# A weight load put behind a transposing transfer, and one group of transposes moved one block earlier, in a fused attention and MLP kernel

## The chip, the cores and the metric

The kernel runs on one core of one Trainium2 chip. Its time is the device time of one launch in microseconds, the median of several runs. The core has five engines that run side by side, each through its own instructions in order: PE (TensorE: matmuls, with weight loads shown apart as PEld), DVE (VectorE), ACT (ScalarE), POOL (GpSimd) and SP (SyncE, here only an issuer of transfers). Transfers are issued from SP's and POOL's queues (a few from ACT's) and carried by 16 DMA engines that all queues share. An engine waits for another engine, or for a transfer, on a semaphore.

## The reference

```python
def _attn_ref(q, k, v, f):
    scores = scale * np.matmul(q, k.transpose(0, 1, 3, 2))
    log_f = np.log(np.clip(f, 0.0001, 1.0))
    cum = np.cumsum(log_f, axis=-1)
    decay = cum[:, :, :, None] - cum[:, :, None, :]
    scores = np.where(causal, -1000000000.0, scores + decay)
    scores = scores - np.max(scores, axis=-1, keepdims=True)
    attn = np.exp(scores)
    attn = attn / (np.sum(attn, axis=-1, keepdims=True) + 1e-09)
    return np.matmul(attn, v)
...
def _moe_ref(x, w_in, w_out):
    h = x @ w_in
    g = 0.5 * h * (1.0 + erf(h * inv_sqrt2))
    return g @ w_out
...
x = attn_out.transpose(0, 2, 1, 3).reshape(B * S, H * D)
return _moe_ref(x=x, **moe_kwargs)
```

q, k and v are (8 batches, 8 heads, 576 tokens, 64 columns) in float32, f is (8, 8, 576). w_in is 512 x 2048 and w_out 2048 x 512. The output has 4608 x 512 numbers in float32. So it is a causal attention with a decay for each token, followed by two matrix products with a gelu between them.

## The kernel before

The kernel goes through the eight batches in order, and works on the heads in four pairs (i = 0 to 3). Within a batch it forms scores for a pair in four tiles in PSUM (`scores`, L299; the matmuls are L319), exponentiates each tile on ACT (L329), masks diagonal blocks on POOL (L331), multiplies by the weighted v (`attend`, L350) and normalizes on DVE (L365, L366). The result, transposed, is xT, the input of the first matrix product. That product (`gemm1`, L437) makes 16 blocks of 128 hidden columns, four matmuls each, and ACT's gelu (L457) turns each into a tile g. The second product (g times w_out, L481, L530, L566 and L590) is spread as filling between the scores of the following batch.

The order is written out by hand: the instructions of an engine stand in the order in which the Python code calls them.

w_out lies in one tile, w_out_sb, loaded in four quarters of 512 KB from POOL's queue (`load_w_out(c)`, L186 to L188). Quarter c holds row blocks 4c to 4c + 3 of the 16. The second product of batch 0 reads blocks 0 to 7 during batch 1's attention (L566), and blocks 8 to 15 at the start of batch 2's attention (L590, in `gemm2_second`).

q and k of batch 0 and batch 1 are transposed by PE (`transposes_first`, L226), 36 small transposes for each pair, and DVE copies the results out of PSUM (L241) into qT and kT. From batch 2 on, transposing transfers issued by SP do it (`transpose_dma`, L255): four for a batch, q and k for heads 0 to 3, then q and k for heads 4 to 7. They write the tiles tq and tk, from which DVE copies (`untangle`, L269) into qT and kT. Behind batch 2's four transfers stand, on SP's queue, the small transposing transfer of batch 1's tail (L422) and the five loads of batch 2's v (L134).

`behind(t, h)` (L613 to L616) puts a small POOL copy that reads one column of t on POOL's queue. POOL waits in it until t has been written, and what POOL issues after it can't start before. The kernel uses it to hold the loads of w_out's quarters 2 and 3 until the k of batch 2 has been loaded.

The places that the change touches are in `second_attention` (batch 1's attention, L912 to L974) and in the loop over batches (L976 to L1013), where batch 0's gemm1 blocks 4 to 9 run with other work put between them. Blocks 10 to 15 of batch 0 are done in batch 1's attention (`gemm1_hold`, L462). Batch 1's first scores need pair 0 transposed. ACT loads another function table when it goes from gelu to exp: a tiny activation at L925, put ahead of the first exp, takes that load. Scores go through two PSUM buffers (pool s_psum), so the third tile waits for the first tile's exp.

Of the kernel before, what the change touches and what calls it, by code (L numbers as in the profile page):

```python
# [18 lines left out]
H = 8  # L19
# [35 lines left out]
def kernel(  # L55
# [130 lines left out]
    def load_w_out(c):  # L186
        kt = slice(c * n_ff // 4, (c + 1) * n_ff // 4)
        nc.gpsimd.dma_start(w_out_sb[:, kt, :], w_out_r[:, kt, :])  # L188
# [28 lines left out]
    def transposes_first(b, i, pool, tag, both=(0, 1), parts=1):  # L217

        half, g = divmod(2 * i, H // 2)
        src = qk_of[b][half]  # L220
        pss = {w: pool.tile([P, J0, D], BF16, tag=tag, name="ps_f") for w in both}
        for j in range(J0):
            for which in both:
                rows = slice(which * D, (which + 1) * D)
                for h in range(2):
                    nc.tensor.transpose(  # L226
                        pss[which][h * D : (h + 1) * D, j, :],
                        src[rows, g + h, j * D : (j + 1) * D],
                        ident_bf[rows, rows],
                    )  # L230

        for which in both:
            dst = (qT, kT)[which][i].rearrange("d (p j) -> d p j", j=J0)
            ps = pss[which].rearrange("d j p -> d p j")
            copies = [nc.vector.tensor_copy] * parts
            if b == i == 0:
                copies = [nc.vector.tensor_copy, nc.scalar.copy]
            n = D // len(copies)
            for at, copy in enumerate(copies):
                part = slice(at * n, (at + 1) * n)  # L240
                copy(dst[:, part], ps[:, part])  # L241

    tq_of = {}
# [39 lines left out]
    def weigh_v(b, i, eng=nc.gpsimd, n0=0, n1=NBLK):  # L283

        hs = slice(2 * i, 2 * i + 2)
        bh = b * H + 2 * i
        w = wT[:, n0:n1, bh : bh + 2].rearrange("p n h -> p h n")
        eng.tensor_tensor(  # L288
            vw(b)[:, hs, n0:n1, 0:D],
            v_sb[:, hs, n0:n1, :],  # L290
            w.unsqueeze(3).to_broadcast([P, 2, n1 - n0, D]),
            Alu.mult,
        )
        if b:
            eng.tensor_copy(vw(b)[:, hs, :, D], w)
# [47 lines left out]
    def attend(b, i, h, ms, pool=o_psum, tag="o"):  # L343
        if (b, i, h) not in o_of:
            o_of[b, i, h] = pool.tile([P, NBLK, D + 1], FP32, tag=tag, name="o")
        o = o_of[b, i, h]
        for m in ms:
            for n in range(m + 1):
                t, c = where(n, m)
                nc.tensor.matmul(  # L350
                    o[:, m, :],
                    e_of[b, i, t][:, h, c : c + P],
                    vw_of[b][:, 2 * i + h, n, :],
                    start=(n == 0),
                    stop=(n == m),
                )

    def normalize(b, i, h):
        if (b, i) not in x_of:
            x_of[b, i] = x_pool.tile([P, NBLK, 2, D], BF16, tag="x", name="x")  # L360
        divide(x_of[b, i][:, 0:NQ, h, :], o_of[b, i, h], NQ)
# [57 lines left out]
    def tail_end(b, o):  # L419
        x = x_pool.tile([P, HP, D], BF16, tag="xt", name="xt")  # L420
        divide(x, o, HP)
        nc.sync.dma_start_transpose(  # L422
            tails[:, :, b].rearrange("d i a t -> d i (a t)"),
            x.rearrange("p k d -> p (k d)"),
        )
# [36 lines left out]
    def gemm1_hold(ffb, copy=nc.vector.tensor_copy):  # L462
        ps = gemm1(0, ffb, act=False)
        h_of[ffb] = h_pool.tile([P, TC], FP32, tag=f"h{ffb}", name=f"h{ffb}")
        copy(h_of[ffb], ps)
# [92 lines left out]
    def gemm2_first(c):  # L558

        pss = [  # L560
            m_psum.tile([P, d_model], FP32, tag="m", name="ps2") for _ in range(2)
        ]
        for kq in (0, 4):
            for ts in range(2):
                for kt in range(kq, kq + 4):
                    nc.tensor.matmul(  # L566
                        pss[ts],
                        g_of[c][kt][:, ts * P : (ts + 1) * P],
                        w_out_sb[:, kt, :],
                        start=(kt == 0),  # L570
                        stop=(kt == 7),
                    )
                    if kt == 7:
                        ot_of.append(
                            o_pool.tile([P, d_model], FP32, tag="ot", name="ot")
                        )
                        copy = nc.scalar.copy if ts else nc.vector.tensor_copy
                        copy(ot_of[ts], pss[ts])
                    yield
# [27 lines left out]
    def take(gen, n):  # L607
        for _ in range(n):
            if next(gen, "end") == "end":
                return  # L610


    def behind(t, h):  # L613

        g = x_pool.tile([P, 1], FP32, tag="gate", name="gate")
        nc.gpsimd.tensor_copy(g[:PT], t[:PT, h, 0:1])  # L616
# [295 lines left out]
    def second_attention():  # L912


        b, fill = 1, gemm2_first(0)

        def av(i, h):
            attend(b, i, h, range(NQ))
            normalize(b, i, h)

        def transposes(i, pool, tag):
            transposes_first(b, i, pool, tag)


        nc.scalar.activation(warm[0:1, 0:1], warm[0:1, 0:1], Act.Exp)  # L925
        def tiles(i, t):
            scores(b, i, t)
            scores(b, i, t + 1)

        def run(i):  # L930
            av(i, 0)
            av(i, 1)

        tiles(0, 0)
        transposes(1, o_psum, "o")
        gemm1_hold(10)
        gemm1_hold(11)
        tiles(0, 2)
        gemm1_hold(12, nc.scalar.copy)
        transposes(2, o_psum, "o")  # L940
        tiles(1, 0)
        gemm1_hold(13)
        run(0)
        tiles(1, 2)
        gemm1_hold(14, nc.scalar.copy)
        transposes(3, o_psum, "o")
        weigh_v(1, 2)
        tiles(2, 0)
        gemm1_hold(15)
        run(1)  # L950
        weigh_v(1, 3)
        tiles(2, 2)
        take(fill, 4)
        tiles(3, 0)
        transpose_dma(2, 0, 4)
        transpose_dma(2, 4, 8)
        to_xT(b, 0, nc.vector.tensor_copy, o_psum, "o")
        to_xT(b, 1, nc.vector.tensor_copy, o_psum, "o")
        take(fill, 4)
        tiles(3, 2)  # L960
        behind(qk_of[2][1], H - 1)
        load_w_out(2)
        load_w_out(3)
        run(2)
        take(fill, 4)
        av(3, 0)
        take(fill, 4)
        both = s_psum.tile([P, 2, 1024], BF16, tag="s", name="ps_x2")
        to_xT(b, 2, nc.scalar.copy, ps=both[:, 0, 0:TC])
        av(3, 1)  # L970
        o = tail(1)
        gemm1_begin(1, both)
        tail_end(1, o)
        load_v(2)  # L974

    for b in range(B):  # L976
        if b == 0:
            first_attention()
        elif b == 1:
            second_attention()  # L980
        else:
            attention(b)
        for ffb in range(4 if b < 2 else 5, n_ff):
            if b == 0 and ffb in HELD:
                continue
            aside = ffb in (8, 9, 12, 13) if b > 1 else b == 1 and ffb % 4 < 2
            if b < 2 or ffb > 6:
                gemm1(b, ffb, ps=spare() if aside else None)
            if b == 1 and ffb % 2 == 0:
                at = HELD[(ffb - 4) // 2]  # L990
                gelu(0, at, h_of[at])
            if b == 0:
                if ffb == 4:
                    attend_tail()
                if ffb == 5:
                    tail_0()
                if ffb == 7:
                    weigh_v(1, 0)
                    load_w_out(0)
                    weigh_v(1, 1)  # L1000
                    load_w_out(1)
                    load_qk_tokens(2)
                if ffb == 8:
                    transposes_first(1, 0, o_psum, "o")
            elif b + 1 < B:
                if b == 1 and ffb == 10:
                    load_qk_tokens(3)
                first, gap = (5, 3) if b == 1 else (1, 4)
                at, late = divmod(ffb - first, gap)
                if late == 0:  # L1010
                    untangle(b + 1, at)
                if late == gap - 2 and (b > 1 or at < 2):
                    weigh_v(b + 1, at)  # L1013
# [34 lines left out]
```

## Time and profile before

| | us |
|---|---|
| median of 3 runs (lowest, highest) | 329.01 (328.47, 330.38) |
| the profiled execution's own time | 330.34 |
| its span, from first to last instruction | 328.4 |
| PE busy | 316.2 |
| ACT busy | 202.5 |
| DVE busy | 176.3 |
| POOL busy | 153.6 |
| PE waiting for other engines or transfers in total, as its table of waits lists them | 7.1 |

All times in the profile count from the start of the span. A timeline row gives the start, the duration, the engine, the line of the code, the operation, the tiles that it writes and reads, the number of instructions merged into the row, and in brackets the time that the engine sat idle before it with what ended that idle time. SPq rows are transfers being issued by SP; their length is the time that SP's queue was held by the issue, not the transfer. The time "to landing" runs from the start of the issue until the data are there. Two tables used for the stage are these: the landing times of w_out's four loads (from the view of that tile), and of tq and tk. They are, as least, median and greatest: 6.5, 7.8 and 10.8 us for w_out_sb, 3.5, 4.0 and 11.2 for tq, 3.5, 3.8 and 7.7 for tk.

The granted TensorE clock is full throughout the span.

### The profile page before, as it was taken

The page shows a single profiled execution, that of the slowest core. Times are in us where ns is not written, and L with a number is a line of the kernel's source. Part 1 is how long each engine was busy: PE and PEld are TensorE (multiplying, and loading weights), DVE is VectorE, ACT ScalarE, POOL GpSimd, SP SyncE. Part 2 cuts the span into 40 slices and gives each one's busy share as a digit, 9 for nine tenths or more (in the row PEclk, how much of TensorE's full clock was granted, in tenths as well). Part 3 has the DMA queues.
Part 4 walks back from the last instruction along what each step waited for, and adds up shares of the span by engine and source line. Part 5 has one row for each costly group of instructions (what it writes and reads, how often), then busy time and mean ns, then how long its engine had stood idle before and what let it go on. Part 6 is the DMA issues. An engine that isn't in the chain of part 4 may idle for free.

```text
span 328.4 us, 8109 instructions
## 1 busy us (share of the span) xinstructions
PE 316.2 (96%) x3308; PEld 168.5 (51%) x3338; DVE 176.3 (54%) x423; ACT 202.5 (62%) x296; POOL 153.6 (47%) x283
## 2 busy tenths in 40 slices
PE   7889999999999999999999999999999989999995
PEld 3664555444464466445644564456545554444443
DVE  5851656763389437982599159914995360010011
ACT  4886885984635895289718980899088916405600
POOL 8987873039306582577336841595059500000000
PEclk9999999999999999999999999999999999999999
DMA  7999999979866959595949683979460141021013
GB/s 122 193 195 219 210 194 146 170 153 173 186 152 166 188 129 135 151 195 104 188 104 212 120 183 76 219 129 188 99 179 2 66 98 40 2 89 38 0 45 85
DMA packets 72294, 43.87 MB, mean 134 GB/s; under 512 B 50081, under 2 KB 65697, under 8 KB 72257
## 3 DMA queue, kind: packets, MB, share of 16 engines
q0 software_dynamic: 18592, 21.89, 38.1%
q1 hardware_dynamic: 53264, 20.93, 29.8%
q8 instruction: 26, 0.43, 0.5%
q10 hardware_dynamic: 400, 0.52, 0.4%
q14 instruction: 12, 0.09, 0.1%
HBM read 36.85 MB, written 9.44 MB: 141 GB/s over the span
## 4 chain that ended last, share of the span: by engine, by line
PE 89%; DMA 4%; ACT 2%; DVE 2%; issue 2%; POOL 0%; SPq 0%; POOLq 0%; DVEq 0%
PE ps L437 38%; PE ps L530 26%; PE ps L481 8%; PE s L319 6%; PE o L350 4%; DMA xT<-x 3%; PE s L640 1%; ACT e L645 1%; PE o L410 1%; PE ps_f L226 1%; DMA q<-in_k_dram 1%; PE ps L590 1%; ACT e L329 1%; DVE x L366 1%; PE ps L566 1%
## 5 line engine op out<-in xcount | busy, mean ns | idle before, releaser
L457 ACT ACTIVATE g<-ps 128x512 bf16<-128x512 f32 x138 | 75.3, 619 | 86.2 <-PE ps L437 85.1
L437 PE MATMUL ps<-xT,w_in_sb 128*128 128x512 bf16 x498 | 112.7, 379 | 2.9 <-DMA xT<-x 1.5
L530 PE MATMUL ps<-w_out_sb,g 64*128 64x512 bf16 (+1 forms) x754 | 104.5, 376 | 0.3
L329 ACT ACTIVATE e<-s 128x896 bf16<-128x896 f32 x112 | 87.8, 836 | 13.2 <-PE s L319 10.9
L437 PEld LDWEIGHTS <-w_in_sb 128*128 128x128 bf16 x576 | 55.1, 98 | 67.9 <-DVE ot L902 2.0
L331 POOL TENSOR_SCALAR_AFFINE_SELECT e<-e 128x256 bf16<-128x256 bf16 (+1 forms) x135 | 48.5, 382 | 29.3 <-ACT e L329 29.2
L530 PEld LDWEIGHTS <-g 64*128 64x128 bf16 (+1 forms) x766 | 42.3, 94 | 30.9
L288 POOL TENSOR_TENSOR vw<-v_sb,wT 128x640 bf16<-128x640 f32 (+1 forms) x30 | 38.0, 1270 | 34.7 <-DMA v_sb<-in_v_dram 31.2
L544 DVE COPY ot<-ps 128x512 f32<-128x512 f32 x20 | 13.8, 692 | 61.5 <-PE ps L530 61.5
L269 DVE COPY kT<-tk 64x288 bf16<-64x288 bf16 x96 | 40.3, 420 | 2.1 <-DMA tk<-k 0.5
L319 PE MATMUL s<-qT,kT 64*128 64x256 bf16 (+1 forms) x336 | 37.8, 275 | 0.8 <-DVE kT L241 0.6
L269 DVE COPY qT<-tq 64x288 bf16<-64x288 bf16 x96 | 34.6, 360 | 3.5 <-DMA tq<-q 2.1
L490 DVE COPY ot<-ps 128x512 f32<-128x512 f32 (+2 forms) x9 | 5.7, 632 | 50.3 <-PE ps L481 50.3
L134 POOL DMA_DIRECT2D v_sb<-in_v_dram x36 | 31.0, 871 | 2.2 <-POOL gate L616 0.8
L319 PEld LDWEIGHTS <-kT 64*128 64x128 bf16 x336 | 18.1, 94 | 20.0 <-issue 4.4
L481 PE MATMUL ps<-w_out_sb,g 128*128 128x512 bf16 (+2 forms) x142 | 27.9, 355 | 0.1
L550 DVE TENSOR_TENSOR ot<-ot,ps 128x512 f32<-128x512 f32 x28 | 19.3, 688 | 4.1 <-remote 2.1
L481 PEld LDWEIGHTS <-g 128*128 128x128 bf16 x144 | 13.5, 98 | 14.5
L350 PEld LDWEIGHTS <-e 128*128 128x128 bf16 x560 | 18.6, 98 | 3.9 <-issue 2.1
L616 POOL CAST gate<-xT 96x1 f32<-96x1 bf16 x5 | 1.3, 267 | 39.8 <-DMA xT<-x 39.8
L350 PE MATMUL o<-vw,e 128*128 128x65 bf16 x560 | 19.8, 194 | 0.2 <-POOL e L331 0.2
L366 DVE TENSOR_TENSOR x<-o,r 128x256 bf16<-128x256 f32 x41 | 17.4, 425 | 1.4
(92 smaller groups left out, 215.1 us busy)
## 6 DMA issues: line engine op xcount, KB each, us to landing
out_dram<-ot SPq DMA_DIRECT2D x32, 256.0 KB, 2.3
v_sb<-in_v_dram POOLq DMA_DIRECT2D x20, 256.0 KB, 4.6
q<-in_q_dram POOLq DMA_DIRECT2D x6, 576.0 KB, 7.6
k<-in_k_dram POOLq DMA_DIRECT2D x6, 576.0 KB, 9.6
v_sb<-in_v_dram POOLq DMA_DIRECT2D x22, 128.0 KB, 5.9
w_in_sb<-in_moe_w_in_dram POOLq DMA_DIRECT2D x4, 512.0 KB, 7.5
w_out_sb<-in_moe_w_out_dram POOLq DMA_DIRECT2D x4, 512.0 KB, 7.8
v_sb<-in_v_dram SPq DMA_DIRECT2D x4, 256.0 KB, 4.1
```

The costliest lines, as they stand in the source:

```text
L134: eng.dma_start(v_sb[p0:P, h0:h1, n, :], v[b, h0:h1, K0[n] + p0 : K0[n] + P].rearrange("h p d -> p h d"),)
L269: nc.vector.tensor_copy(rows[:, odd], src[odd * D : (odd + 1) * D, 2 * i + h].rearrange("d j p -> d p j"),)
L288: eng.tensor_tensor(vw(b)[:, hs, n0:n1, 0:D], v_sb[:, hs, n0:n1, :], w.unsqueeze(3).to_broadcast([P, 2, n1 - n0, D]), Alu.mult,)
L319: nc.tensor.matmul(to, *ab, start=half < 0, stop=half == 1 or not masked)
L329: nc.scalar.activation(et[:, :, z:c], st[:, :, z:c], Act.Exp, scale=scale)
L331: nc.gpsimd.affine_select(out=et[:, :, c0 + z : c0 + P], in_=et[:, :, c0 + z : c0 + P], compare_op=Alu.is_ge, fill=0.0, base=z, pattern=[[ ...
L350: nc.tensor.matmul(o[:, m, :], e_of[b, i, t][:, h, c : c + P], vw_of[b][:, 2 * i + h, n, :], start=(n == 0), stop=(n == m),)
L366: nc.vector.tensor_tensor(x, o[:, 0:n, 0:D], r[:, 0:n].unsqueeze(2).to_broadcast([P, n, D]), Alu.mult,)
L437: nc.tensor.matmul(ps, w_in_sb[:, kt, ffb * P : (ffb + 1) * P], xT(c)[:, kt, 0:TC] if c < B else tails[:, kt % 2, :, kt // 2, :], start=(k ...
L457: nc.scalar.activation(g_of[c][ffb], ps, Act.Gelu)
L481: nc.tensor.matmul(pss[ts][:, c0:c1], g_of[c][kt][:, ts * P : (ts + 1) * P], w_out_sb[:, kt, c0:c1], start=(kt == 0), stop=(kt == n_ff - 1),)
L530: nc.tensor.matmul(banks[r], g_of[c][kt][rows, ts * P : (ts + 1) * P], w_out_sb[rows, kt, :], start=kt == 0, stop=last if r else kt == n_f ...
```

## The change

One line is added in `second_attention`: after quarter 2 of w_out has been issued, a `behind` on the last heads of batch 2's tk, ahead of quarter 3. In the batch loop a condition is taken out, so that the transposes of batch 1's pair 0 stand after block 7 of batch 0's gemm1 (and after the POOL work listed there), and no longer after block 8.

```diff
         tiles(3, 2)
         behind(qk_of[2][1], H - 1)
         load_w_out(2)
+        behind(tq_of[2][1].rearrange("d h j p -> d h (j p)"), H - 1)
         load_w_out(3)
         run(2)
...
                     weigh_v(1, 1)
                     load_w_out(1)
                     load_qk_tokens(2)
-                if ffb == 8:
                     transposes_first(1, 0, o_psum, "o")
             elif b + 1 < B:
```

`tq_of[2]` is the pair of tiles (tq, tk) of batch 2, so `tq_of[2][1]` is tk, and its heads 4 to 7 are written by the last of the four transposing transfers.

In the built programs the instructions are otherwise the same: POOL has one more copy (the gate); SP's later transfer into tk (batch 3's) gets a wait for that copy; on PE the 36 transposes stand ahead of the four matmuls of block 8 where they stood behind them. The second `behind` waits for the one semaphore of that transposing transfer, and PE's first matmul with row block 12 waits for the semaphore of quarter 3 alone.

## The prediction

> **What bounds the kernel now.** I read first the page's busy times and its chain of waits, then the table of what TensorE (PE) waited for, then each engine's timeline at the two edited places.
>
> ```profile
> PE 316.2 (96%) x3308; PEld 168.5 (51%) x3338; DVE 176.3 (54%) x423; ACT 202.5 (62%) x296; POOL 153.6 (47%) x283
> ...
> PE 89%; DMA 4%; ACT 2%; DVE 2%; issue 2%; POOL 0%; SPq 0%; POOLq 0%; DVEq 0%
> ```
>
> PE is the bound: 316.2 of 328.4 us busy, and 89% of the chain. A change can save only PE's few idle gaps, and any new gap in PE is paid in full. The table of PE's waits (in total, times, longest) names the one gap at the second edit:
>
> ```profile
> PE s L319 <- DVE kT L241: 0.6, 1, 0.6
> PE s L319 <- ACT e L329: 0.2, 1, 0.2
> ```
>
> The 0.6 us is batch 1's first score matmul waiting for the copy of the transposed k of pair 0. Nothing in that table names w_out or the transposing transfers (tq, tk) of batch 2: what the first edit touches costs PE nothing today.
>
> **Edit 2, the transposes one block sooner.** It adds nothing and moves 36 PE transposes and their two DVE copies (L241) ahead of block 8's four matmuls. PE's and ACT's timelines there (start, duration, then the idle time before):
>
> ```profile
> 31.56 0.48 PE L226 MATMUL ps_f<-key_of,q 64*64 64x64 bf16 x36
> 33.63 0.28 PE L319 MATMUL s<-qT,kT 64*128 64x256 bf16 x2 [0.63 <-DVE kT L241]
> ...
> 36.82 0.30 PE L319 MATMUL s<-qT,kT 64*128 64x320 bf16 x2
> ```
> ```profile
> 33.04 0.60 ACT L457 ACTIVATE g<-ps 128x512 bf16<-128x512 f32 x1 [0.78 <-PE ps L437]
> 33.66 1.28 ACT L925 ACT_TABLE_LOAD   x1
> 34.95 0.21 ACT L925 ACTIVATE warm<-warm 1x1 bf16<-1x1 bf16 x1
> 35.06 1.58 ACT L329 ACTIVATE e<-s 128x896 bf16<-128x896 f32 x2
> 37.02 1.51 ACT L329 ACTIVATE e<-s 128x896 bf16<-128x896 f32 x2 [0.38 <-PE s L319]
> ```
>
> Four L437 matmuls last 0.86 us on PE, so the transposes start at 31.56 - 0.86 = 30.7, the copies end 0.86 earlier, at 33.58 - 0.86 = 32.7, and the scores can start when block 9 ends, at 33.0: the 0.63 us gap goes. Their inputs are there: POOL's wait for the load of that half of q and k ended at 29.07, and the last reader of the same PSUM buffers, the copy at L715, ended at 29.26. No DMA moves.
>
> But little of the 0.63 reaches the end. PE's work up to the end of block 9 is the same, so the gelu of block 9 still starts at 33.04, the table load and the first exp (35.06) stay where they are. The second pair of score tiles needs the buffers of the first two exps, which end at about 35.9 and 35.06 + 1.58 = 36.64. The fourth tile started at 36.82 and cannot start before 36.64 + 0.05, so PE is ahead by 36.82 - 36.69 = 0.13 us from there on: 0.5 us of gap moves to a wait for ACT. Block 8's gelu moves 0.48 later, within the 0.78 us that ACT then idles. Bounds: 0 if ACT holds all of it, 0.63 if the exps don't hold PE. I take **-0.13 us**.
>
> **Edit 1, w_out's last quarter behind tk.** It adds one POOL copy of 96x1 (0.18 us, the row at 50.69) and a wait, and moves one 512 KB load on POOL's queue. POOL's, SP's and PE's timelines:
>
> ```profile
> 50.69 0.18 POOL L616 CAST gate<-k 96x1 f32<-96x1 bf16 x1 [0.20 <-DMA k<-in_k_dram]
> 50.81 1.56 POOL L188 DMA_DIRECT2D w_out_sb<-in_moe_w_out_dram  x2
> 71.02 1.28 POOL L288 TENSOR_TENSOR vw<-v_sb,wT 128x640 bf16<-128x640 f32 x1 [18.65 <-DMA v_sb<-in_v_dram]
> ```
> ```profile
> 51.97 4.50 SPq L255 DMA_TRANSPOSE tq<-q  x1
> 56.51 5.25 SPq L255 DMA_TRANSPOSE tk<-k  x1
> 61.80 1.25 SPq L422 DMA_TRANSPOSE tails<-xt  x1
> 63.31 4.39 SPq L134 DMA_DIRECT2D v_sb<-in_v_dram  x5
> ```
> ```profile
> 67.33 1.89 PE L590 MATMUL ps<-w_out_sb,g 64*128 64x512 bf16 x16
> ```
>
> Behind the new wait stand on POOL only the load itself and then L288, which waits for v until 71.02 anyway. The next transposing transfer into tk gets a wait for the gate's read; it is issued at 86 us, some 24 us past it. So the one thing at stake is when the quarter lands against its first reader. That is row block 12: L590 starts at 67.33 with block 8 and reaches block 12 after 8 of 16 matmuls (1.73 us in the chain), at 67.33 + 0.87 = 68.2; with edit 2's 0.13, **68.1**.
>
> *Today:* issued at 51.6, and the w_out tile's longest landing is 10.8 us, so 62.4: 5.8 us to spare.
>
> *When tk lands.* Issue plus time to landing gives tq's second half 51.97 + 11.2 = 63.17 (DVE's copy of it starts at 63.19) and tk's second half 56.51 + 7.7 = 64.2. The first half of tk landed at 57.05 (DVE's copy starts then). In the DMA view, microsecond by microsecond, the software queue carried 0.53 MB from 57 to 62, the size of the last quarter, while the transposes crept. Alone (55 to 57) it moved 0.17 to 0.20 MB per us, so without it 2.7 to 3.1 us go: tq 60.1 to 60.5, tk 1.0 later, 61.1 to 61.5. The other way: tk's first half moved its 0.3 MB in 1.9 us while alone (51.7 to 53.6), so tq could land at 57.05 + 1.9 + 0.3 (for its closing writes, which in tk's second half came in from 63.9 to 64.2) = 59.3 and tk at 60.3. I take **60.9**, between them.
>
> *When the quarter lands.* Gate and issue follow a landing by 0.3 us (50.5 to 50.81): issue at 61.2. The four w_out loads took 6.5 to 10.8 us; the two of this stage have a median of 9.2, so the other took 2 x 9.2 - 10.8 = 7.6. That one is the nearest row: first in its queue, with transposes beside it, as this one will have the v loads beside it. 61.2 + 7.6 = **68.8**, so PE stalls 68.8 - 68.1 = **0.7 us**. Bounds: 60.3 + 0.3 + 6.5 = 67.1, no stall; 61.5 + 0.3 + 10.8 = 72.6, a stall of 4.5 us (that 10.8 had another load ahead of it, so I weigh it little). After 68 us PE runs without a gap to the next batch, so the stall passes on whole.
>
> [...]
>
> What the edit gives back: tq and tk land about 3 us sooner, and so do the tails transfer and the v loads queued behind them on SP. PE waits for none of these: DVE loses its 2.06 us wait at 63.19, but its copies were done at 68.6 and their scores come at 82; v's product is first read at 91.8 (L350), 20 us after POOL starts it. If that cover were gone the gain would be up to 3 us, but nothing in PE's waits asks for it.
>
> **Sum.** -0.13 + 0.7 = +0.5 to +0.6 us on the profiled execution: span 328.4 to 329.0, its time 330.34 to 330.9. That execution lies 1.33 above the median of the three runs (329.01), within their spread (328.47 to 330.38); from the median the forecast is **329.5 us**, no change by the measure of 0.5% (1.65 us), below which a measurement of this kernel can't tell a difference.
>
> **Rivals.**
> *The quarter is in time* (landing before 68.1): tk at 60.3 and a load of 6.5 to 7.5 us. For: DMA carries little after 64 in today's trace but v. Against: v moves up into the same microseconds. Only edit 2 is left: 329.01 - 0.13 = **328.9**.
> *The quarter lands with v, late* (the slower one): SP gets to the five v loads at about the time of the gate, and today their data take 63.3 to 70.0, 6.7 us. Started at 61.0 beside 0.52 MB more (2.6 us at 0.2 MB per us) all is in at about 70.3. If the quarter finishes only with them, PE stalls 70.3 - 68.1 = 2.2 us: **331.1**. It decides from a landing 1.8 us past need. For: tk's first half moved its last bytes by 54 beside the w_out load and counted as landed only at 57.05. Against: against the transposes the software queue kept 0.16 MB per us, four fifths of its pace alone.
> [...]
> *The whole of edit 2, and more*: 0.63 is kept, and the two waits of PE for xT (1.5 us in the table of waits) happen to vanish: 326.9. Nothing in the change touches the latter.
>
> **Numbers.** Forecast (stall up to 1.8 us) 0.46; in time 0.25; with v 0.24; faster 0.05. Faster by over 0.5%: 0.05; within: 0.71 (the first two); slower: 0.24. The range goes from 328.2 (in time, less the 0.54 by which the lowest run lies under the median, rounded down) to 331.9 (with v, and 0.8 of the 1.4 by which the highest run lies above it).
>
> **What would show it.** PE's timeline: no idle at the first L319 of batch 1, a wait on ACT (L329) near 36.0 to 36.7 in its place; then one idle gap inside L590 at 68, released by DMA w_out_sb, of 0 to 2 us. POOL: a second L616 row at 60.3 to 61.5 with L188 behind it. SP: L255 of tk ending near 59 and v starting near 61. It is wrong if the L590 gap is over 2.5 us, or if tk lands after 62.

## The result and the profile after

| | before | after |
|---|---|---|
| median of 16 runs each (us) | 329.31 | 332.59 |
| lowest and highest | 328.36, 333.17 | 330.78, 336.36 |
| ratio after to before, 95% interval | | 1.0083 [1.0058, 1.0108] |
| the profiled execution's own time | 330.34 | 332.41 |
| its span | 328.4 | 330.4 |

The change made the kernel slower by 0.83%, which is 2.7 us (1.9 to 3.6 by the interval). The forecast was no change, +0.5 us, to 329.5 us, in a range that ended at 331.9. Ratios here and below leave out executions in a slower state, while medians, lowest and highest keep them, so a ratio and a quotient of medians can differ. Edit 1 is the new gate ahead of w_out's last quarter, edit 2 the transposes one block sooner.

The first place to look is the chain of waits of the changed kernel, in the stretch from 39 to 72 us (start, duration, what the chain was held by; three issue steps of 0.04 us and less are left out):

```profile
39.09 12.29 DMA k<-in_k_dram
51.39 1.28 SPq L255
52.72 3.43 SPq L255
56.19 6.21 DMA tk<-k
62.40 0.06 issue
62.45 0.26 POOL gate L616
62.71 8.36 DMA w_out_sb<-in_moe_w_out_dram
71.07 0.04 issue
71.11 1.04 PE ps L590 x8
```

In the first profile of the kernel before, this stretch of the chain is nearly all PE's own work, and L590 runs through:

```profile
67.19 0.30 PE s L319 x4
67.49 1.73 PE ps L590 x16
```

Now the chain goes through the load of k, the transposing transfers, the new gate, the load of the last quarter and back to PE's L590: each of those steps delays the next, and PE comes last. The page's shares of the chain can't be used to show this. PE has 76% and DMA 12% after the change, against 89% and 4% in the first profile of before; but a second profile of the kernel before (below) has 74% and 14%, because a wait of 0.35 us at L530 leads its chain through tq's transfer and DVE's copies. What only kernels with the new gate have is the wait inside L590. The timelines of PE and then POOL at the two edited places:

```profile
34.12 0.28 PE L319 MATMUL s<-qT,kT 64*128 64x256 bf16 x2
...
37.88 0.31 PE L319 MATMUL s<-qT,kT 64*128 64x320 bf16 x2 [0.24 <-ACT e L329]
...
68.39 1.03 PE L590 MATMUL ps<-w_out_sb,g 64*128 64x512 bf16 x8
71.11 1.04 PE L590 MATMUL ps<-w_out_sb,g 64*128 64x512 bf16 x8 [1.69 <-DMA w_out_sb<-in_moe_w_out_dram]
```

```profile
51.51 0.18 POOL L616 CAST gate<-k 96x1 f32<-96x1 bf16 x1
51.63 0.83 POOL L188 DMA_DIRECT2D w_out_sb<-in_moe_w_out_dram  x1
62.45 0.33 POOL L616 CAST gate<-tk 96x1 f32<-96x1 bf16 x1 [10.00 <-DMA tk<-k]
62.71 0.75 POOL L188 DMA_DIRECT2D w_out_sb<-in_moe_w_out_dram  x1
```

Edit 2 did what it says: the 0.63 us before the first L319 of batch 1 is gone, and a wait for ACT of 0.24 us stands before the fourth tile. Edit 1 did what it says too: the last L188 has moved from 51.6 to 62.71, and PE, after the eight matmuls of blocks 8 to 11, sits idle for 1.69 us until the quarter is there.

In this execution PE also ran at half clock from 11.2 to 18.0 us, before either edit can act. That made PE 1.2 us late by 30 us, and so 1.06 us late at L590 (68.39 against 67.33). It makes the gap look small: PE came late to a load that was later still. Two more profiles of this kernel and one of edit 1 alone show 3.7 to 3.9 us (below).

### The profile page after: what moved, and what is told of

Read it like the earlier page. It is cut to its first block, busy times and chain, and to the rows that moved or that the text cites. A ratio compares the mean times of both kernels' runs of the same rounds, so it can differ in the third digit from the quotient of the medians.

```text
span 330.4 us, 8139 instructions
## 1 busy us (share of the span) xinstructions
PE 321.2 (97%) x3338; PEld 171.9 (52%) x3338; DVE 173.2 (52%) x423; ACT 202.9 (61%) x296; POOL 153.8 (47%) x284
## 4 chain that ended last, share of the span: by engine, by line
PE 76%; DMA 12%; POOL 8%; SPq 1%; issue 1%; DVE 0%; POOLq 0%
PE ps L437 29%; PE ps L530 27%; PE ps L481 8%; PE s L319 5%; PE o L350 4%; DMA k<-in_k_dram 4%; DMA q<-in_k_dram 3%; DMA w_out_sb<-in_moe_w_out_dram 3%; DMA tk<-k 2%; POOL v_sb L169 2%; SPq L255 1%; POOL vw L288 1%; POOL v_sb L134 1%; DMA xT<-x 1%; PE o L410 1%; POOL q L120 1%
## 5 line engine op out<-in xcount | busy, mean ns | idle before, releaser
L437 PE MATMUL ps<-xT,w_in_sb 128*128 128x512 bf16 x512 | 114.0, 379 | 0.3 <-DMA xT<-x 0.2
L530 PE MATMUL ps<-w_out_sb,g 64*128 64x512 bf16 (+1 forms) x766 | 107.2, 376 | 0.0
L437 PEld LDWEIGHTS <-w_in_sb 128*128 128x128 bf16 x576 | 55.1, 98 | 66.9 <-issue 2.0
L530 PEld LDWEIGHTS <-g 64*128 64x128 bf16 (+1 forms) x766 | 43.6, 94 | 29.6
L288 POOL TENSOR_TENSOR vw<-v_sb,wT 128x640 bf16<-128x640 f32 (+1 forms) x30 | 38.8, 1293 | 27.7 <-DMA v_sb<-in_v_dram 27.7
L319 PE MATMUL s<-qT,kT 64*128 64x256 bf16 (+1 forms) x336 | 38.1, 275 | 0.5 <-ACT e L329 0.4
L269 DVE COPY kT<-tk 64x288 bf16<-64x288 bf16 x96 | 35.8, 373 | 2.3 <-DMA tk<-k 0.7
L269 DVE COPY qT<-tq 64x288 bf16<-64x288 bf16 x96 | 35.1, 366 | 1.5
L319 PEld LDWEIGHTS <-kT 64*128 64x128 bf16 x336 | 18.6, 94 | 19.4 <-issue 4.3
L550 DVE TENSOR_TENSOR ot<-ot,ps 128x512 f32<-128x512 f32 x28 | 19.3, 688 | 4.1 <-PE ps L530 2.1
L366 DVE TENSOR_TENSOR x<-o,r 128x256 bf16<-128x256 f32 x41 | 17.4, 425 | 1.4
```

The source lines that it names most:

```text
L269: nc.vector.tensor_copy(rows[:, odd], src[odd * D : (odd + 1) * D, 2 * i + h].rearrange("d j p -> d p j"),)
L288: eng.tensor_tensor(vw(b)[:, hs, n0:n1, 0:D], v_sb[:, hs, n0:n1, :], w.unsqueeze(3).to_broadcast([P, 2, n1 - n0, D]), Alu.mult,)
L319: nc.tensor.matmul(to, *ab, start=half < 0, stop=half == 1 or not masked)
L437: nc.tensor.matmul(ps, w_in_sb[:, kt, ffb * P : (ffb + 1) * P], xT(c)[:, kt, 0:TC] if c < B else tails[:, kt % 2, :, kt // 2, :], start=(k ...
L530: nc.tensor.matmul(banks[r], g_of[c][kt][rows, ts * P : (ts + 1) * P], w_out_sb[rows, kt, :], start=kt == 0, stop=last if r else kt == n_f ...
L550: nc.vector.tensor_tensor(ot, ot, bank, Alu.add)
```

## The experiments

All are edits of the changed kernel, except where the diff says otherwise. Gaps are PE's idle time inside L590.

| | ratio to before [95%] | issue of the last quarter, us | gap, us |
|---|---|---|---|
| changed kernel | 1.0083 [1.0058, 1.0108] | 62.71 | 1.69 |
| the same again, twice | one run each, 333.23 and 335.64 us | 63.25 and 63.35 | 3.66 and 3.89 |
| edit 1 alone | 1.0116 [1.0073, 1.0159] | 63.23 | 3.90 |
| edit 2 alone | 0.9987 [0.9952, 1.0023] | 53.4 (no gate) | none |
| gate on tk's first half | 1.0019 [0.9988, 1.0050] | 59.14 | none |
| gate on tq's second half | 1.0009 [0.9982, 1.0037] | 61.80 | 1.32 |
| v from POOL's queue, behind the quarter | 1.0076 [1.0051, 1.0100] | 63.25 | 0.69 |
| v held on SP until the quarter is in | 1.0106 [1.0045, 1.0166] | 63.38 | 0.62 |
| the quarter read later | 1.0082 [1.0054, 1.0110] | 63.36 | 1.75 |
| quarters 2 and 3 gated early, v held | 1.0062 [1.0039, 1.0085] | 56.2 | none |
| edit 2, last copies of L269 later | 1.0073 [1.0047, 1.0099] | 52.8 (no gate) | none |

### Each edit alone

Edit 1 alone puts the condition `ffb == 8` back:

```diff
                     load_qk_tokens(2)
+                if ffb == 8:
                     transposes_first(1, 0, o_psum, "o")
```

> The gate ahead of w_out's last quarter alone; batch 1's first transposes stay behind block 8. Theory A (the loss is PE waiting for the quarter in its first reader, L590): L590 shows an idle gap of 1.5 to 3.5 us released by the w_out load, PE's 0.6 us wait for kT is back, and the time is 329.3 + 2.7 + 0.1 = about 332.1 us. Rival B (the moved transposes are what costs): about 329.3 us, no gap in L590.

Measured: 333.16 us (median of 6), ratio 1.0116. Its PE timeline:

```profile
66.76 1.03 PE L590 MATMUL ps<-w_out_sb,g 64*128 64x512 bf16 x8
71.68 1.89 PE L590 MATMUL ps<-w_out_sb,g 64*128 64x512 bf16 x8 [3.90 <-DMA w_out_sb<-in_moe_w_out_dram]
```

Edit 2 alone takes the gate out:

```diff
         load_w_out(2)
-        behind(tq_of[2][1].rearrange("d h j p -> d h (j p)"), H - 1)
         load_w_out(3)
```

> The transposes one block sooner alone; both w_out quarters as before. Theory A: 0.13 us less than before, about 329.2 us, indistinguishable from it; no 0.6 us wait for kT, a wait of some 0.2 us for the exp at L329 in its place, no gap in L590. Rival B (the moved transposes cost): 331 to 333 us.

Measured: 329.52 us (median of 12), ratio 0.9987, no gap in L590, no wait for kT. So the loss is edit 1's, and it is the gap: all of it goes with the gate. Edit 2's own 0.13 us is smaller than this measurement can tell (its interval is 2.3 us wide).

The row of 1.89 us for eight matmuls behind the gap of edit 1 alone, where the same eight take 1.04 in the changed kernel, was the first sign of a second cost, which the repeats below show.

### How late the quarter may be issued

Two kernels move the gate to an earlier transfer: to tk's first half, which is the second of the four transposing transfers, and to tq's second half, the third.

```diff
-        behind(tq_of[2][1].rearrange("d h j p -> d h (j p)"), H - 1)
+        behind(tq_of[2][1].rearrange("d h j p -> d h (j p)"), H // 2 - 1)
```

> Both edits, but the gate reads the heads 0 to 3 of tk, which land some 5 us before heads 4 to 7. Theory A: the quarter is issued near 57 to 58, lands by 67 and is in time for block 12 at about 68.1; no gap in L590, about 329.2 us. Rival C (the extra gate on POOL's queue costs, or the order of the loads does, not the landing): the loss stays, 331 to 333 us.

```diff
-        behind(tq_of[2][1].rearrange("d h j p -> d h (j p)"), H - 1)
+        behind(tq_of[2][0].rearrange("d h j p -> d h (j p)"), H - 1)
```

> Both edits, but the gate reads tq's heads 4 to 7 (the third of the four transposing transfers) and no longer tk's. In the changed kernel tq lands some 1.0 to 1.5 us before tk. Theory A: the quarter is issued and lands 1.0 to 1.5 us sooner, the gap in L590 falls from 3.7 (its second profile) to about 2.4 us, the clock is seldom halved, and the time is 331.0 to 331.5 us, between the gate on the first half (330.0) and the changed kernel (332.6). Rival C (the gate on POOL itself costs): as the changed kernel, 332.6.

Measured: 329.98 us (12 runs, ratio 1.0019) with an issue at 59.14 and no gap, and 330.25 us (12 runs, ratio 1.0009) with an issue at 61.80 and this:

```profile
68.78 1.04 PE L590 MATMUL ps<-w_out_sb,g 64*128 64x512 bf16 x8 [1.32 <-DMA w_out_sb<-in_moe_w_out_dram]
```

With the gate still there and only its place changed, the loss is gone, so an extra gate on POOL's queue costs nothing by itself that this measurement can see. The gap grows with the issue: none at 59.1, 1.32 at 61.8, 1.69 at 62.7 (where PE was late) and 3.66 to 3.90 at 63.2 to 63.4. In the profile of the gate on tk's first half the quarter landed at 66.2 and block 12 was reached at 68.5, 2.3 us to spare; but PE had waited 1.60 us there for an earlier load (at L226, see the repeats below), so an execution without that wait has less. With the gate on tq the load took 7.0 us (61.80 to 68.75), against 8.4 in the changed kernel. Neither kernel's time can be told from before. The gap of 1.32 less edit 2's 0.13 us would be 0.36%, at the upper end of the interval; one profile doesn't say how long the gap is in the other runs.

### Is it v that slows the quarter?

The prediction's slower rival held that the quarter and batch 2's v, issued in the same microsecond, would land together. Two kernels take v out of the quarter's way. The first issues v from POOL's queue, behind the quarter:

```diff
         tail_end(1, o)
-        load_v(2)
+        load_v(2, eng=nc.gpsimd)
```

> Both edits, and batch 2's v is loaded from POOL's queue behind the quarter, no longer from SP's beside it. Theory A1 (the sharing of the DMA engines with the v loads makes the quarter late): it lands 6 to 7 us after its issue where the changed kernel took 8.4, so the gap in L590 falls from 1.7 to 0 to 0.5 us and the time to 329.2 to 330. Theory A2 (the issue after tk alone is too late): landing still 8 us or more after issue, gap 1.5 to 3 us, about 332 us. The product with v is read 18 us later, so a later v should cost nothing in either.

The second holds SP's v loads until the quarter has landed: POOL waits for it in one more gate, and then writes one column of the tile that v goes to.

```diff
         load_w_out(3)
+        behind(w_out_sb, n_ff - 1)
+        nc.gpsimd.memset(v_sb[:, :, 0, 0:1], 0.0)
         run(2)
```

> Both edits; v waits on SP until the last quarter has landed, so that neither the DMA engines nor POOL's descriptor work for v stand beside the quarter or the L269 copies. Theory A1 (sharing with v makes it late by nearly 3 us): landing 5.5 to 6.5 us after issue, gap 0 to 0.8, no stretched L269 copies, 329.3 to 330.3 us. Rival A2 (the issue after tk is too late by itself): landing 8 us or more, 332 us.

Measured: in both, the quarter came in 5.3 to 5.5 us after its issue (63.25 to 68.8, 63.38 to 68.7), against 8.0 to 9.0 beside v. So v costs the quarter some 2.5 to 3.7 us, and without it the gap falls to 0.69 and 0.62. But the time did not come down: ratios 1.0076 and 1.0106, the latter from the lower three of six runs (330.72, 333.15 and 334.93; the others took 336.07 to 336.85, at a granted clock of 0.990). Where it went is in their traces. With v on POOL's queue, DVE's row, POOL's and then PE's:

```profile
64.14 1.89 DVE L269 COPY kT<-tk 64x288 bf16<-64x288 bf16 x4
```

```profile
63.98 4.55 POOL L134 DMA_DIRECT2D v_sb<-in_v_dram  x5
```

```profile
72.82 0.37 PE L530 MATMUL ps<-w_out_sb,g 64*128 64x512 bf16 x1 [0.88 <-DVE ot L598]
```

DVE's copies of tq and tk take 1.34 us for four while POOL is idle. Beside POOL's issues of the quarter and of v they take 1.50, 1.89 and 1.88. They also began late in this execution, the first of tk at 61.23 against 58.06 to 60.52 in the changed kernel's three profiles, because k landed late (gate at 52.69). So DVE reaches the sums L598 and L550 late, and PE waits for the PSUM buffers that these free: 0.88 and 0.35 us. How much of that is due to each of the two isn't separated. With v held on SP, PE and POOL later on:

```profile
101.36 2.97 PE L437 MATMUL ps<-xT,w_in_sb 128*128 128x512 bf16 x13 [3.01 <-DMA xT<-x]
```

```profile
77.81 1.28 POOL L288 TENSOR_TENSOR vw<-v_sb,wT 128x640 bf16<-128x640 f32 x1 [8.76 <-PE s L319]
...
80.56 0.84 POOL L120 DMA_DIRECT2D q<-in_q_dram  x1
```

v is issued at 69.08, 6 to 7 us later than in the changed kernel (61.91 to 62.69), so L288 is late, and behind L288 on POOL's queue stand the loads of batch 3's q and k (L120), at 80.56 where they were issued at 74 to 75 before and at 76 to 77 in the changed kernel. From them on it is taken to be a train: in the first profile of the kernel before, SP issues the transposes of batch 3 from 84.64 and the xT transfers behind them from 93.62, so late loads would make both late. Of this kernel the two ends are measured, the loads at 80.56 and PE's wait of 3.01 us for xT at 101; the steps between are the author's estimate.

So the sharing with v is real (5.3 to 5.5 us against 8.0 to 9.0), and neither way of moving v brought the time down.

### Reading the quarter later

Instead of the load, this one moves the need: `gemm2_second` takes blocks 8 to 11 of both row tiles, then 12 to 15 of both.

```diff
-            for kt in range(8, n_ff):
-                for r in range(2):
...
+        for kq in (8, 12):
+            for ts in range(2):
+                banks = banks_of[ts]
+                for kt in range(kq, kq + 4):
+                    for r in range(2):
```

> Both edits as in the changed kernel; the first product with blocks 8 to 15 (L590) takes blocks 8 to 11 of both row tiles ahead of blocks 12 to 15 of both, so the quarter is first read 1.05 us later (8 matmuls and 4 score matmuls). Theory A: the gap shrinks by about 1.0 us and the time by as much or a little more (where the clock is halved after a long gap), 331.0 to 331.8 us. Rival C (something else in the late load's train costs): no change, 332.6.

Measured: a gap of 1.75 us, in the same product (L593 in this kernel). Its first read of block 12 moved to 69.80, 1.05 us later than without the reordering. The sums of the two row tiles now come together, and PE waits 0.25 us for L550 at L530, which the changed kernel doesn't. The time, 332.32 us (6 runs, 1.0082), is no lower than the changed kernel's, whose gaps vary from 1.7 to 3.9. On the time this is inconclusive.

### Both quarters early, and v behind them

```diff
-        behind(qk_of[2][1], H - 1)
+        behind(tq_of[2][1].rearrange("d h j p -> d h (j p)"), H // 2 - 1)
         load_w_out(2)
-        behind(tq_of[2][1].rearrange("d h j p -> d h (j p)"), H - 1)
         load_w_out(3)
+        behind(w_out_sb, n_ff - 1)
+        nc.gpsimd.memset(v_sb[:, :, 0, 0:1], 0.0)
```

> Edit 2 kept; both quarters wait for tk's heads 0 to 3 (so all transposes have few loads beside them), and batch 2's v waits on SP until the last quarter has landed. If the loss of the changed kernel is only the quarter's landing against block 12, and if the copies out of tq and tk (L269) were near to delaying the sums (L598, L550) in the kernel before: tk's heads 0 to 3 land near 54 to 56, the quarters near 61 and 64, no gap in L590, the L269 copies end by 66.5, no wait for the sums in L530, and 328.5 to 329.3 us, at or a little under the kernel before. If a late v or a late first store costs: a wait for v or for the output tiles, 330 us or more.

Measured: 331.08 us (12 runs), ratio 1.0062, and no gap in L590. But the second half of tk now shares the transfers with 1 MB of weights and lands 10.2 us after its issue; DVE waits for it:

```profile
65.48 1.34 DVE L269 COPY kT<-tk 64x288 bf16<-64x288 bf16 x4 [4.22 <-DMA tk<-k]
```

That costs PE 0.35 us at L530. Another 0.93 us go to a wait for xT at 98.5, where the two profiles of the kernel before have none; the late v, by the same train as in the kernel with v held on SP, is the likely cause, but no run here takes it away.

### Is the copy's lateness worth a change by itself?

In edit 2 alone, and in a second profile of the kernel before (below), PE loses 0.35 to 0.53 us at L530 to DVE's sums, because the last L269 copies end just ahead of these. This kernel (edit 2 without the gate) moves the last pair's copies into batch 2's attention:

```diff
                 if b == 2 and (i, t) == (0, 3):
+                    untangle(2, 3)
...
-                if late == 0:
+                if late == 0 and (b > 1 or at < 3):
                     untangle(b + 1, at)
```

> Edit 2 alone, and the last pair's copies out of tq and tk of batch 2 (L269, 2.7 us of DVE) put behind the first sums of batch 0's second product. If PE's waits for those sums (0.18 and 0.35 us in the profile of edit 2 alone) come from the L269 copies ahead of them on DVE, they go, and the time is 328.9 to 329.3 us, 0 to 0.5 under the kernel before. If not, they stay or another copy (L544) is late in their place: 329.5 or more.

Measured: 332.64 us (9 runs), ratio 1.0073: a miss. The waits at L598 went, but DVE's copies, in their new place beside POOL's products and issues, took 4.6 and 2.2 times as long, and PE waited 3.46 us:

```profile
74.99 6.11 DVE L269 COPY qT<-tq 64x288 bf16<-64x288 bf16 x4
81.11 2.97 DVE L269 COPY kT<-tk 64x288 bf16<-64x288 bf16 x4
```

```profile
84.86 0.37 PE L530 MATMUL ps<-w_out_sb,g 64*128 64x512 bf16 x1 [3.46 <-DVE ot L544]
```

### The same kernels again

The kernel before was profiled once more and the changed kernel twice, to see how much one profile's margin is worth. No edit.

> The kernel before, unaltered, for a second sight of where PE and the transfers stand against each other: L590 starts at 66.2 to 66.8 where PE's early part runs at the full clock (the first profile's 67.3 would be a late one), k of batch 2 lands at 51 to 52.5 (the first profile's 50.5 an early one), and the last quarter lands at 62 to 64, 4 us or so ahead of block 12.

> The changed kernel unaltered, for a second sight of the gap's size. [...]

> The changed kernel unaltered, a third sight. If the transfers and not PE set the moment: the quarter lands at 71.0 to 71.7 as in the earlier profiles (71.1, 71.2), whatever time PE reaches L590, and the gap is that less PE's arrival at block 12.

Measured: before 329.19 us, changed 333.23 and 335.64. The kernel before, PE:

```profile
66.03 1.89 PE L590 MATMUL ps<-w_out_sb,g 64*128 64x512 bf16 x16
...
70.72 1.88 PE L530 MATMUL ps<-w_out_sb,g 64*128 64x512 bf16 x15 [0.35 <-DVE ot L550]
```

PE is at L590 1.3 us earlier than in the first profile of the same kernel (67.33), and the k gate is 0.41 later (51.10 against 50.69). The quarter, issued at 52.0 with a longest landing of 11.0, was in at 63.0, and block 12 is reached at 66.9: 3.9 us to spare, not 5.8. This execution also has the 0.35 us at L530, which none of the four profiles with the gate on tk (three of the changed kernel, one of edit 1 alone) has: with tk earlier, DVE's copies are done in time.

The changed kernel's third profile, PE's timeline and then two windows (length, then busy time of PE, PEld, DVE, ACT and POOL, the granted clock, DMA share and GB/s):

```profile
67.49 1.03 PE L590 MATMUL ps<-w_out_sb,g 64*128 64x512 bf16 x8
72.40 1.46 PE L590 MATMUL ps<-w_out_sb,g 64*128 64x512 bf16 x8 [3.89 <-DMA w_out_sb<-in_moe_w_out_dram]
73.94 3.08 PE L590 MATMUL ps<-w_out_sb,g 64*128 64x512 bf16 x16
```

```profile
72.00:74.00 2.00, 1.60 (x14) 0.83 (x15) 0.10 (x1) 0.00 (x0) 0.00 (x0) 0.72 0.23 46
74.00:76.00 2.00, 2.00 (x12) 0.88 (x10) 1.27 (x2) 0.81 (x1) 1.64 (x3) 0.50 0.03 8
```

The clock column falls to 0.50 shortly after PE resumes, and the sixteen matmuls at 73.94 take 3.08 us in place of 1.89. It stays at half for 3.4 us (72.9 to 76.3), and at half speed that is about 1.7 us of work lost, on top of the gap. Edit 1 alone shows the same from 71.7 to 75.1. After the gaps of 1.69 and 3.66 us the clock stayed full.

Both repeats have one more wait that neither profile of the kernel before and not that of edit 1 alone has: 0.66 and 1.43 us at L226, ahead of 37.35 and 38.27 us, for a load of batch 1's k. In the other profiles of kernels with edit 2 it ranges from nothing to 1.60 us. It lies before the gate can act; it makes PE later at L590 and so shortens the gap, but not the time. Whether edit 2 brings it on or the load varies by itself is not shown. Edit 2 alone was at most 0.23% slower than before, by its interval.

## Why the prediction was wrong

The mechanism was the one forecast: a single gap inside L590, released by the last quarter, passed on whole (in the second profiles of the two kernels, PE is 4.4 us apart at the scores behind the first L590, 74.01 against 69.65, and the spans are 4.1 us apart). Its size was not. The step that failed is the one that set the quarter's landing at 68.8 against a need at 68.1, for a stall of 0.7 us. The quarter landed at 71.1 to 72.4 and was needed at 67.6 to 69.4, which makes stalls of 1.7 to 3.9 us. The signs that the prediction gave for being wrong both appeared: tk landed after 62 in all four profiles (62.40 to 63.18), and the gap was over 2.5 us in three.

Counted from the k gate, which marks the landing of k that starts the whole train of transfers, the terms of four profiles with the new gate can be laid beside the prediction's. The quarter's landing is where PE resumes, the need is that less the gap:

| us after the k gate | predicted | changed | again | again | edit 1 alone |
|---|---|---|---|---|---|
| k gate itself | 50.69 | 51.51 | 51.75 | 52.06 | 51.76 |
| gate on tk | 10.3 | 10.9 | 11.4 | 11.2 | 11.4 |
| quarter landed | 18.1 | 19.6 | 19.5 | 20.3 | 19.9 |
| block 12 reached | 17.4 | 17.9 | 15.9 | 16.5 | 16.0 |
| gap | 0.7 | 1.7 | 3.7 | 3.9 | 3.9 |

- **When tk lands** was 0.6 to 1.1 us too early against the k gate. Taking the quarter out of the transposes' way did shorten them: tk landed 13.6 us after the landing of k before (13.7 in the second profile), 11.0 after (62.40 less 51.39; 11.2 to 11.4 in the other three). That is at most 2.6 of the 2.7 to 3.1 us that the first of the two reckonings gave, and its end (61.1 to 61.5) was the better one; the value taken, 60.9, was pulled down by the second reckoning. On top of that k itself landed 0.8 to 1.4 us later than in the first profile of before, which alone would not have mattered had PE been as late.
- **The load** was priced at 7.6 us by the nearest row, and took 8.36, 8.0, 9.0 and 8.4. That row had transposes beside it; this load had v, and v costs it more: without v it takes 5.3 to 5.5. The five v issues on SP, for their part, held the queue for 7.36 us in place of 4.39. The rival "lands with v, late" had this sharing with v, with a stall of 2.2 us, and was the nearer one, though the quarter did not land only with v: L288's wait for v ended at 73.19, 2.1 us after the quarter. The prediction's argument against it was misread: the software queue's 0.16 MB per us beside the transposes is that of a single microsecond, and 0.53 MB in the five from 57 to 62 is 0.11, about half of its pace alone.
- **The need** was read from one execution. There PE was late (67.33 at L590) and the transfers early, which gave 5.8 us of slack; the second profile of the same kernel gives 3.9. Against the k gate block 12 came at 17.5 us in the first profile of before and at 15.8 in the second. In this stretch nothing in these profiles ties the two trains: the transfers run from the landing of k, and PE from its own work. What made PE late in the first profile is only partly seen: its table of waits has 0.8 us at L226 for the loads of k at the kernel's start, and 1.4 us at L640 with no cause shown ("issue"), which the second lacks. The profiled execution was known to lie 1.33 us above the median; the forecast moved its base to the median for that, but left the need where that execution had it.
- **The clock** was no term at all. Of four profiles with the gate two, with gaps of 3.89 and 3.90, lost some 1.7 us more to 3.4 us of half clock. The mean granted clock of each run says how common that is: 3.4 us at half clock in 333 us bring it to 0.995. It was 0.995 or less in 6 of the changed kernel's 16 runs (mean 333.6 us, against 332.0 for the other ten; one of the six is the first profile, where the clock fell at 11.2 us) and in 4 of the 6 of edit 1 alone, but in only 2 of 65 runs of the kernel before made beside the experiments, and in none of the 12 of edit 2 alone.
- **Together**: gaps of 1.7 to 3.9 (mean 3.3), 0.8 us for the clock on average, less edit 2's 0.1 and less the 0.35 at L530 that the gate gives back, make some 3.6 us. The measured differences are 2.7 us [1.9, 3.6] for the change and 3.8 [2.4, 5.2] for edit 1 alone. Three of the four profiled executions took longer than the median of their kernel (333.23 and 335.64 against 332.59, 335.32 against 333.16), so their mean overstates the loss; four profiles don't fix it more closely.
- **Edit 2** was right in each step. The wait for kT went, the exps held the fourth tile for 0.24 us, and 0.13 was left: in the changed kernel's first profile PE came to L590 1.06 us late, having been 1.19 late at the end of batch 0's tail, and edit 2 alone, against the second profile of before, went from 0.52 late there to 0.39 at the fourth tile. The times are too coarse to show it.
- **"If that cover were gone"**: the prediction gave v 20 us of cover, and expected nothing from DVE's copies ending sooner. Each missed a path. Behind v's product on POOL's queue stand the L120 loads, and with v late by 6 us PE waited 3.0 us at 101. And the L269 copies end so close to DVE's sums that PE waits 0.35 us for these in the second profile of before, a wait that the gate takes away. Neither decided the result, but each undid an attempt to mend it.
- **The smaller waits** for xT, which the rival "the whole of edit 2, and more" played with, fell to 0.2 us in the changed kernel's first profile from 1.5, and were 0.9 and 0.6 in its other two and 0.4 in the second profile of before. Edit 1 alone has 1.4 and edit 2 alone 1.3, so they vary without following either edit.
- **Two slips** change nothing: k landed at 50.63 (issued at 38.43, 12.2 us to landing) and not at 50.5, and 328.9 less 0.54 is 328.4, where the range was made to start at 328.2.

None of the versions tried is faster than the kernel before. Three of them (edit 2 alone, and the two earlier gates) cannot be told from it.

## What to carry to other kernels

A margin between two trains of work that nothing ties together (here a load that follows transfers, and a matmul that follows PE's own work) is not what one profile shows: look at several executions before moving a load later, and count both trains from the event that starts them. A load that is moved is to be priced beside what will run next to it in its new place, not what ran next to it in the old. And a stall can cost more than its length: here 3.4 us at half clock, some 1.7 us of work, came on top of stalls of 3.46, 3.89 and 3.90 us, though not of one of 3.66.

## What the runs showed of the hardware

- **Half clock after a gap.** Gaps in PE of 3.89, 3.90 and, in the kernel with the later copies, 3.46 us were each followed, 0 to 1.1 us after PE resumed, by 3.4 us at a granted clock of 0.5; gaps of 3.66 and 1.69 us were not. So the length of a gap alone doesn't decide it. What does is not shown.
- **Copies beside POOL.** Four DVE copies of 64x288 bf16 took 1.34 us with POOL idle, up to 1.89 beside POOL's issuing of five loads, and 6.11 beside POOL's products, selects and issues. Why the copies take longer there is not shown.
- **A casting load alone and in company.** 512 KB of w_out (counted as stored) came in after 5.3 to 5.5 us without v beside it, 7.0 to 9.0 with, and up to 11.0 behind another quarter with transposes beside it.
